# Sparse attention with routed experts: blocks of values on every fourth partition, exponentials written in the matching order, one GpSimd copy of values a tile

## The chip, the cores and the metric

One core of one Trainium2 chip. The metric is the device time of one execution in microseconds; the kernel before took 536.8 us (median of three runs, 534.89 to 540.84). A profiled execution gives the trace from which everything below is read.

## The reference, cut to what matters

Block-sparse attention over 4 batches of 8 heads, 768 positions and 64 channels, in blocks of 32 positions, and then a mixture of 8 experts in which each token goes to one expert:

```python
mask = np.abs(blk_i - blk_j) <= 1
mask = mask | (blk_i == 0) | (blk_j == 0) | (blk_i == n_blocks - 1) | (blk_j == n_blocks - 1)
for qb in range(n_blocks):
    for kb in sampled_blocks[qb]:
        mask[qb * 32:(qb + 1) * 32, kb * 32:(kb + 1) * 32] = True
scores = np.where(mask, scale * q @ k.T, -1e9)
attn = softmax(scores); out = attn @ v
...
e_idx = argmax(x @ w_gate + modality_bias[modality_id])
out[mask] = gate_w[mask, None] * (np.maximum(x[mask] @ w1[e], 0.0) @ w2[e])
```

So a middle block of queries sees eight blocks of keys and values: its own, its two neighbours, the first, the last, and three that are drawn (22 of the 24 blocks of queries are of this kind; the first and the last see everything).

## The kernel before, in words

**Halves and tiles.** The four batches are two halves of two. In each half the 22 middle blocks of queries are 11 tiles of two neighbouring blocks i and i+1 (i = 2m+1); tile g = 11 * half + m, so there are 22 sparse tiles. Blocks 0 and 23 of queries form the dense items. After the attention come groups of 256 tokens for the experts; that part starts at about 240 us and the change leaves it alone.

**Values of a tile.** `vbuf[g % 2]` holds 128 partitions by three columns of 1024 numbers (two batches, eight heads, 64 channels). A block of values is 32 rows of 4 KB and takes 32 partitions of one column. Column 1 is seen by both blocks of queries: i, 0, 23 and i+1. Column 0 belongs to the first block of queries: its three drawn blocks and i-1. Column 2 belongs to the second: i+2 and its three drawn blocks. Before, a block lay on 32 neighbouring partitions (0-31, 32-63, 64-95, 96-127).

**How they come there.** `fetch_v` (L484) issues, on SP's queue, the loads of i+2 (L495) and i+1 (L496), and for the first two tiles of a half the blocks 0 and 23 (L490); a half's first tile loads four more (L492, L493). `share_v` (L499) has GpSimd copy two blocks from the tile before: its i+1 becomes the new i-1, its i+2 the new i (two operations on 32 partitions by 1024 at L503). `fetch_own` (L515) loads the three drawn blocks of a block of queries, n = 0 into column 0 or n = 1 into column 2 (L520); the block numbers are registers read on SP (L512). Every load on SP waits for the one issued eight loads earlier, since eight counters are used in turn.

**Keys.** `share_k` (L461) has GpSimd copy the blocks of keys (L465, L469, and twelve copies at L481).

**One item.** An item is one block of queries (n) of one batch of one tile, four to a tile. Its steps: scores on TensorE (L532); mask and minimum on VectorE, which writes `y` (L540); two exponentials on ScalarE, which write `a` with the sum (L548, 256 numbers a partition each); four transposes on TensorE (L557); the copy to `at` on ScalarE (L562). After a tile's four items, TensorE multiplies with the values: `weigh_shared` (L574, matmuls at L579, column 1) and `weigh_own` (L582, L588, columns 0 and 2). A transposed row of `at` must lie on the same partition as its row of values. Then come division (L439 to L441), the transposes of the result (L595), its copy (L597) and the router (L605).

**What sets the order.** PE, DVE, ACT, POOL and SP run a hand-written order. A clock `t` counts items; `LAG` says how many places behind its item a step runs (`weigh_shared` 5 and `weigh_own` 7 behind the tile's last item), and within a place there are eight spots. `VL = (8, 1)`, `VS = (11, 7)` and `VG = ((9, 6), (10, 3))` (L69 to L71) place `fetch_v`, `share_v` and `fetch_own` n = 0 and n = 1: so many items behind the last item of tile g-2, and the spot. An engine's own instructions run in this order; where one waits, all behind it on that engine wait. The tile framework adds the waits that the buffers need.

Of the kernel before, what the change touches and what calls it, by code (L numbers as in the profile page):

```python
# [14 lines left out]
AF = mybir.ActivationFunctionType  # L15
ALU = mybir.AluOpType
# [4 lines left out]
P = 128  # L21
# [45 lines left out]
KL = (-2, 2)  # L67
QP = (-2, 2)
VL = (8, 1)  # L69
VS = (11, 7)  # L70
VG = ((9, 6), (10, 3))  # L71

DENSE_IN = ((19, 14, 30), (49, 38, 44))
Q_IN = 22
# [14 lines left out]
def attention_moe(ctx, tc, kD, qD, qH, v0, v1, blocks, modality, w_gate, bias, w1, w2, out):  # L89
    nc = tc.nc  # L90
# [28 lines left out]
    with ExitStack() as actx:  # L119
# [336 lines left out]
        def key_numbers(g):  # L456
            i = 2 * (g % NM) + 1
            picked[g] = nc.values_load_multi_w_load_instructions(
                rb_i[0:1, 3 * i:3 * i + 6], [ET.Pool], min_val=0, max_val=NB - 1, skip_runtime_bounds_check_because=NO_CHECK)[1]
# [24 lines left out]
        def fetch_v(m, half):  # L484
            i, g = 2 * m + 1, half * NM + m
            vg = vbuf[g % 2]
            vrow = vH[half].rearrange("(j s) b f -> s j (b f)", s=BLK)
            if m < 2:
                for n, j in ((0, 0), (1, NB - 1)):
                    nc.sync.dma_start(vg[32 + 32 * n:64 + 32 * n, 1, :], vrow[:, j, :])  # L490
            if m == 0:
                nc.sync.dma_start(vg[0:32, 1:3, :], vrow[:, i:i + 3:2, :])  # L492
                nc.sync.dma_start(vg[96:P, 0:2, :], vrow[:, i - 1:i + 2:2, :])  # L493
                return
            nc.sync.dma_start(vg[0:32, 2, :], vrow[:, i + 2, :])  # L495
            nc.sync.dma_start(vg[96:P, 1, :], vrow[:, i + 1, :])  # L496


        def share_v(m, half):  # L499
            g = half * NM + m  # L500
            new, old = vbuf[g % 2], vbuf[(g - 1) % 2]
            for r, c in ((slice(96, P), 0), (slice(0, 32), 1)):
                nc.gpsimd.tensor_scalar(new[r, c, :], old[r, c + 1, :], 1.0, 1.0, ALU.mult, ALU.mult)  # L503
            g = max(picked) + 1
            if g < 2 * NM:
                key_numbers(g)
# [8 lines left out]
        def fetch_own(m, half, n):  # L515
            i, g = 2 * m + 1, half * NM + m
            vg = vbuf[g % 2]
            vrow = vH[half].rearrange("(j s) b f -> s j (b f)", s=BLK)
            for k, reg in enumerate(own[g][3 * n:3 * n + 3]):
                nc.sync.dma_start(vg[32 * (k + n):32 * (k + n) + 32, 2 * n, :], vrow[:, bass.ds(reg, 1), :].rearrange("p j f -> p (j f)"))  # L520

# [21 lines left out]
        def exps(total, y, mn):  # L545
            a = work.tile([P, 768], F32, name="a", bufs=5)[:, 0:512].rearrange("p (u k) -> p u k", u=2)
            for u in range(2):
                nc.scalar.activation(a[:, u, :], y[:, u, :], AF.Exp, bias=mn[:, u:u + 1], scale=-1.0, accum_out=total[:, u:u + 1])  # L548
            return a


# [636 lines left out]
        for k, it in enumerate(sparse[0] + sparse[1]):  # L1188
            items.append(it)
            if k in DENSE_AFTER:  # L1190
                c = 2 * DENSE_AFTER.index(k)
# [5 lines left out]
        def side(t, f, place=7):  # L1197
            work_at.setdefault((t, place), []).append(f)
# [58 lines left out]
        for g in range(2 * NM):  # L1257
            half, m = divmod(g, NM)
            t = at["s", half, m, 0, 0]
            kl = lambda m=m, half=half: q_load(m, half)  # L1260
            qp = lambda m=m, half=half: share_k(m, half)
            vl = lambda m=m, half=half: fetch_v(m, half)
            vg = [lambda m=m, half=half, n=n: fetch_own(m, half, n) for n in range(2)]
            if g < 2:
                loads.update({f"kl{g}": kl, f"qp{g}": qp, f"vl{g}": vl, "vs1": lambda: share_v(1, 0), **{f"v{n}{g}": vg[n] for n in range(2)}})
                continue
            kt = last(g - 2) + KL[0]
            pt = max(kt, t + QP[0])
            vt = last(g - 2) + VL[0]
            side(kt, kl, KL[1])  # L1270
            side(pt, qp, QP[1])
            side(vt, vl, VL[1])
            if m:
                side(last(g - 2) + VS[0], lambda m=m, half=half: share_v(m, half), VS[1])
            for n in range(2):
                side(last(g - 2) + VG[n][0], vg[n], VG[n][1])

        st, done = {}, set()

        def do(op, it):  # L1280
# [29 lines left out]
            else:  # L1310
# [6 lines left out]
                elif op == "M":  # L1317
                    st[it] = masked(m, n, b, st[it])
                elif op == "X":
                    if (n, b) == (0, 0):  # L1320
                        sums[m, half] = small.tile([P, 4, 2], F32, name="sums", bufs=4)
                    st[it] = exps(sums[m, half][:, 2 * b + n, :], *st[it])
                elif op == "T":
                    st[it] = transposed(n, st[it])
                elif op == "A":
                    if n == 0:
                        ats[m, half, b] = work.tile([P, 16, 2, 32], F32, name="at", bufs=NAT)
                    copied(n, b, st.pop(it), ats[m, half, b])
                    if (n, b) == (1, HB - 1):
                        sums[m, half] = spread(sums[m, half])  # L1330
                elif (n, b) == (1, HB - 1):
                    if op == "W":
                        st[it] = bank()
                        weigh_shared(half * NM + m, st[it], [ats[m, half, b_] for b_ in range(HB)])
                    elif op == "V":
                        banks[m, half] = bank()
                        sum_rows(sums.pop((m, half)), banks[m, half])
                        weigh_own(half * NM + m, st[it], [ats[m, half, b_] for b_ in range(HB)])
                    elif op == "O":
                        new_tile(m, half)  # L1340
                        divide(st.pop(it), banks.pop((m, half))[:, 0:H], slice(0, P), H, xrs[m, half][:, 0:HD])
                    elif op == "Y":
                        turns[m, half] = turned(xrs[m, half])
                    elif op == "G":
                        end_tile(m, half)

        man = tc.manual_schedule(engines=MAN) if MAN else ExitStack()
        with man:
# [16 lines left out]
            while t < NI + LAG["s"]["G"] + 1 or fillers or slots_todo or choosers or early:  # L1365
                spot = 0
                for op in ORDER:
# [3 lines left out]
                    for kind in "ds":  # L1371
                        k = t - LAG[kind][op]
# [18 lines left out]
        total = nc.values_load(grp[0:1, 23:24], min_val=NG, max_val=NGMAX, skip_runtime_bounds_check_because=NO_CHECK)  # L1391
# [52 lines left out]
```

## Time and profile before

| what | value |
|---|---|
| median of three runs | 536.8 us (534.89 to 540.84) |
| the profiled execution's own time | 536.03 us |
| its span, first to last instruction | 534.3 us |
| granted TensorE clock, mean | 0.987 |
| busy over the span: PE, DVE, ACT, POOL | 514.9, 377.2, 335.2, 214.9 us |
| SP's transfers (queue q1) | 105.02 MB |
| drawn and shared blocks of values of 128 KB each | 180 transfers, 4.0 us from issue to landing (median) |

How to read it. PE is TensorE's matmuls and PEld its weight loads, which overlap; DVE is VectorE, ACT ScalarE, POOL GpSimd, SP the queue that issues the loads. Matmuls are pipelined and their ends are modelled, so a wait shows best as a gap between starts. "issue" as what ended a wait means that the profile shows nothing that the engine waited for. A window's row gives each engine's busy time and number of instructions in a stretch of the span, then the granted clock, the mean busy share of the sixteen DMA engines and what they moved.

### The profile page before, as it was taken

Reading aid. Unit: us, or ns where it says so; the run is one execution under the profiler, and the core shown is the slowest. Engines: PE = TensorE matmul, PEld = TensorE weight load, DVE = VectorE, ACT = ScalarE, POOL = GpSimd, SP = SyncE. Lnnn points to the kernel's source line nnn. Section 1 sums busy time; section 2 is a strip of 40 time slices with the busy share of each in tenths; the row PEclk is TensorE's granted clock in tenths of the full one; section 3 lists DMA queues with packets and bytes.
Section 4 is the critical chain, followed back from the end, with each engine's and each line's share of the span. In section 5 each row is a group of like instructions: output and inputs, shape, how many; then the busy total and the mean of one; then the engine's idle time right before and its main releaser. Section 6 shows DMA issues by size and latency. Waiting matters only on the chain.

```text
span 534.3 us, 19017 instructions
## 1 busy us (share of the span) xinstructions
PE 514.9 (96%) x7298; PEld 436.1 (82%) x7298; DVE 377.2 (71%) x1139; ACT 335.2 (63%) x765; POOL 214.9 (40%) x451
## 2 busy tenths in 40 slices
PE   7999999998999999899999999999999999999995
PEld 5667776766778777788989898998989899898984
DVE  7995698683788999867997656556565655656553
ACT  4689877884988878835456554546555454655552
POOL 3577685574468884323155022030302203030213
PEclk9999999997999999899999999999999999999998
DMA  7995887898846798965888686676758677675840
GB/s 278 339 234 153 238 244 224 243 229 223 232 126 194 198 231 252 274 193 200 238 288 303 227 261 200 237 252 202 244 177 261 203 227 242 213 246 180 257 155 23
DMA packets 49443, 119.44 MB, mean 224 GB/s; under 512 B 7744, under 2 KB 8128, under 8 KB 49344
## 3 DMA queue, kind: packets, MB, share of 16 engines
q1 hardware_dynamic: 45248, 105.02, 64.5%
q0 software_dynamic: 4096, 13.12, 7.3%
q8 instruction: 59, 0.97, 0.8%
q14 instruction: 40, 0.33, 0.2%
HBM read 105.52 MB, written 12.86 MB: 222 GB/s over the span
## 4 chain that ended last, share of the span: by engine, by line
issue 40%; PE 39%; DVE 7%; DMA 6%; POOL 6%; SPq 2%; ACT 1%; POOLq 0%; DVEq 0%; ACTq 0%
PE bank L557 7%; PE bank L532 6%; PE bank L579 4%; PE bank L588 4%; POOL slot L735 3%; DMA out<-slot,si 2%; DMA slot<-kD 2%; PE bank L605 2%; POOL out L789 2%; PE bank L595 2%; DVE y L540 2%; PE bank L753 1%; PE bank L769 1%; PE bank L770 1%; PE bank L768 1%
## 5 line engine op out<-in xcount | busy, mean ns | idle before, releaser
L724 DVE TENSOR_TENSOR slot<-slot 128x1024 fp32r<-128x1024 f32 x99 | 123.1, 1248 | 89.3 <-ACT slot L721 87.5
L721 ACT CAST slot<-slot 128x1024 fp32r<-128x1024 f32 x104 | 108.1, 1048 | 102.1 <-PE bank L754 52.1
L753 PE MATMUL bank<-slot 128*128 128x256 f32 x384 | 108.4, 282 | 0.0
L755 PE MATMUL bank<-slot 128*128 128x256 f32 x384 | 107.8, 281 | 0.0
L754 PE MATMUL bank<-slot 128*128 128x256 f32 x384 | 107.7, 280 | 0.0
L789 POOL DMA_INDIRECT out<-slot,si x20 | 25.4, 1270 | 178.6 <-ACT slot L785 175.6
L548 ACT ACTIVATE a<-y,mn 128x256 f32<-128x256 f32 x176 | 88.7, 511 | 7.7 <-DVE mn L540 7.6
L768 PE MATMUL bank<-slot 128*128 128x512 f32 x192 | 76.6, 399 | 0.0
L769 PE MATMUL bank<-slot 128*128 128x512 f32 x192 | 75.9, 395 | 0.0
L770 PE MATMUL bank<-slot 128*128 128x512 f32 x192 | 75.8, 395 | 0.0
L753 PEld LDWEIGHTS bank<-slot 128*128 128x128 f32 x384 | 72.3, 188 | 0.6
L754 PEld LDWEIGHTS bank<-slot 128*128 128x128 f32 x384 | 72.1, 188 | 0.4
L755 PEld LDWEIGHTS bank<-slot 128*128 128x128 f32 x384 | 72.2, 188 | 0.0
L540 DVE CUSTOM_DVE_ANT_1 y<-bank,smask 128x256 f32<-128x256 f32 x176 | 66.3, 416 | 0.6 <-PE bank L532 0.2
L481 POOL COPY slot<-slot 128x128 f32 x264 | 63.9, 294 | 0.0
L562 ACT COPY at<-bank 128x512 f32<-128x512 f32 x88 | 50.6, 576 | 12.8 <-PE bank L557 12.7
L557 PE MATMUL bank<-ident,a 128*128 128x128 f32 x352 | 52.8, 284 | 0.6 <-ACT a L400 0.5
L503 POOL TENSOR_SCALAR slot<-slot 32x1024 f32<-32x1024 f32 x40 | 41.9, 1048 | 28.0 <-PE bank L588 10.2
L532 PE MATMUL bank<-slot,q_raw 64*32 64x256 f32 x1408 | 48.8, 382 | 1.1 <-DMA q_raw<-qH 0.7
L770 PEld LDWEIGHTS bank<-slot 128*128 128x128 f32 x192 | 36.1, 188 | 8.4
L557 PEld LDWEIGHTS bank<-ident,a 128*128 128x128 f32 x352 | 38.9, 142 | 4.7 <-ACT a L548 0.8
L769 PEld LDWEIGHTS bank<-slot 128*128 128x128 f32 x192 | 36.1, 188 | 7.8 <-DVE slot L724 0.4
(302 smaller groups left out, 855.4 us busy)
## 6 DMA issues: line engine op xcount, KB each, us to landing
slot<-w SPq DMA_DIRECT2D x100, 512.0 KB, 4.0
slot<-v SPq DMA_DIRECT2D x180, 128.0 KB, 4.0
x_d<-xr SPq DMA_DIRECT2D x22, 256.5 KB, 5.3
q_raw<-qH SPq DMA_DIRECT2D x22, 256.0 KB, 4.8
slot<-v SPq DMA_DIRECT2D x16, 256.0 KB, 4.9
slot<-kD SPq DMA_DIRECT2D x13, 256.0 KB, 4.2
slot<-v SPq DMA_DIRECT2D x4, 768.0 KB, 11.9
slot<-w SPq DMA_DIRECT2D x10, 256.0 KB, 5.1
```

Source lines behind the costliest of these rows:

```text
L532: nc.tensor.matmul(sp[u][32 * pr:32 * pr + 32, b * 256:(b + 1) * 256], lhsT=q[r, b * NPAIR + pr, n, :], rhs=kv[r, s0:s0 + 8, b, pr, :], st ...
L540: nc.vector.tensor_tensor_reduce(y[:, u, :].rearrange("p (s f) -> p s f", s=8), sp[u][:, b * 256:(b + 1) * 256].rearrange("p (s f) -> p s ...
L548: nc.scalar.activation(a[:, u, :], y[:, u, :], AF.Exp, bias=mn[:, u:u + 1], scale=-1.0, accum_out=total[:, u:u + 1])
L557: nc.tensor.transpose(tp[:, k:k + P], a[:, u, c * P:(c + 1) * P], ident)
L721: nc.scalar.copy(h, s)
L724: (eng or (nc.gpsimd if n in POOL_SPLITS else nc.vector)).tensor_tensor(l, s, h.bitcast(F32), ALU.subtract)
L753: nc.tensor.matmul(o, lhsT=h[:, fs], rhs=xh[g % 2][:, c, :], start=c == 0 and f % 2 == 0, stop=False)
L754: nc.tensor.matmul(o, lhsT=h[:, fs], rhs=xl[g % 2][:, c, :], start=False, stop=False)
L755: nc.tensor.matmul(o, lhsT=l[:, fs], rhs=xh[g % 2][:, c, :], start=False, stop=c == 3 and f % 2 == 1)
L768: nc.tensor.matmul(o, lhsT=hh[0][:, f, ts_], rhs=h[:, fs], start=f == 0, stop=False)
L769: nc.tensor.matmul(o, lhsT=hh[0][:, f, ts_], rhs=l[:, fs], start=False, stop=False)
L770: nc.tensor.matmul(o, lhsT=hl[f // 4][:, f % 4, ts_], rhs=h[:, fs], start=False, stop=f == 7)
```

## The change

Three things, which belong together.

- **Place of a block.** A block of values takes partitions s, s+4, s+8, ... (s = 0 to 3) and not 32 neighbours. All value loads now write `vg[s:P:4, ...]`. Block i+1 lies on s = 3 of column 1, which is where i-1 of the next tile must lie in column 0.
- **Order of the exponentials.** For the transposed rows to meet these partitions, each exponential writes its 128-wide halves with the place within a block outside and the slot of the block inside: it reads `y` in order (slot, place) and writes element (slot, place) at 4 * place + slot. Consecutive elements of an instruction are so written 16 bytes apart, and the next slot fills the gaps.
- **Copy and loads.** `share_v` is one copy of all 128 partitions of column 1 of the tile before into column 0 of the new tile. Only the quarter s = 3 of it is used, the drawn blocks of n = 0 are loaded over the rest; so these loads must come behind the copy. Block i is no longer copied but loaded, in one transfer with i+2. `VS` moves to (9, 1), `VG` to (10, 5) for n = 0 and (9, 6) for n = 1.

Lines behind `fetch_v` have numbers lower by one or two in the changed kernel.

```diff
-VS = (11, 7)
-VG = ((9, 6), (10, 3))
+VS = (9, 1)
+VG = ((10, 5), (9, 6))
...
             if m < 2:
                 for n, j in ((0, 0), (1, NB - 1)):
-                    nc.sync.dma_start(vg[32 + 32 * n:64 + 32 * n, 1, :], vrow[:, j, :])
+                    nc.sync.dma_start(vg[1 + n:P:4, 1, :], vrow[:, j, :])
+            nc.sync.dma_start(vg[0:P:4, 1:3, :], vrow[:, i:i + 3:2, :])
             if m == 0:
-                nc.sync.dma_start(vg[0:32, 1:3, :], vrow[:, i:i + 3:2, :])
-                nc.sync.dma_start(vg[96:P, 0:2, :], vrow[:, i - 1:i + 2:2, :])
+                nc.sync.dma_start(vg[3:P:4, 0:2, :], vrow[:, i - 1:i + 2:2, :])
                 return
-            nc.sync.dma_start(vg[0:32, 2, :], vrow[:, i + 2, :])
-            nc.sync.dma_start(vg[96:P, 1, :], vrow[:, i + 1, :])
+            nc.sync.dma_start(vg[3:P:4, 1, :], vrow[:, i + 1, :])
...
             new, old = vbuf[g % 2], vbuf[(g - 1) % 2]
-            for r, c in ((slice(96, P), 0), (slice(0, 32), 1)):
-                nc.gpsimd.tensor_scalar(new[r, c, :], old[r, c + 1, :], 1.0, 1.0, ALU.mult, ALU.mult)
+            nc.gpsimd.tensor_scalar(new[:, 0, :], old[:, 1, :], 1.0, 1.0, ALU.mult, ALU.mult)
...
-                nc.sync.dma_start(vg[32 * (k + n):32 * (k + n) + 32, 2 * n, :], vrow[:, bass.ds(reg, 1), :].rearrange("p j f -> p (j f)"))
+                nc.sync.dma_start(vg[k + n:P:4, 2 * n, :], vrow[:, bass.ds(reg, 1), :].rearrange("p j f -> p (j f)"))
...
-                nc.scalar.activation(a[:, u, :], y[:, u, :], AF.Exp, bias=mn[:, u:u + 1], scale=-1.0, accum_out=total[:, u:u + 1])
+                nc.scalar.activation(a[:, u, :].rearrange("p (c f s) -> p c s f", c=2, s=4), y[:, u, :].rearrange("p (c s f) -> p c s f", c=2, s=4), AF.Exp, bias=mn[:, u:u + 1], scale=-1.0, accum_out=total[:, u:u + 1])
```

How the built program moves. GpSimd first, around the third tile (g = 2); `slot_100` and `slot_101` are the two buffers of values, `slot_98` and `slot_99` those of keys; a row of L465 opens the keys of a tile, L469 follows, and the twelve copies at L481 that close them are left out. Before:

```order
L465 TENSOR_SCALAR slot_99<-slot_98 128x512 [waits PE_49,Pool_49]
...
L465 TENSOR_SCALAR slot_98<-slot_99 128x512 [waits PE_49,Pool_49]
...
L469 TENSOR_SCALAR slot_98<-slot_109 128x2x2x64
...
L503 TENSOR_SCALAR slot_100<-slot_101 32x1024 [waits DMAHW2_49,PE_49,Pool_49]
L503 TENSOR_SCALAR slot_100<-slot_101 32x1024 [waits DMAHW1_49]
L458 TENSOR_LOAD rb_i_141
```

and with the change:

```order
L465 TENSOR_SCALAR slot_99<-slot_98 128x512 [waits PE_49,Pool_49]
...
L501 TENSOR_SCALAR slot_100<-slot_101 128x1024 [waits DMAHW3_49,DMAHW6_49,DMAHW2_49,DMAHW7_49,DMAHW0_49,PE_49]
L458 TENSOR_LOAD rb_i_141
L465 TENSOR_SCALAR slot_98<-slot_99 128x512 [waits Pool_49]
L469 TENSOR_SCALAR slot_98<-slot_109 128x2x2x64
```

One copy stands where two stood, and it stands ahead of the keys of tile 4, behind which the two stood.

SP's queue at the same tile, before (each L520 row is the first of three loads, the other two left out with the steps that set their registers):

```order
L495 DMA slot_100<-v0 32x1024 [waits DMAHW3_49,PE_49,Pool_49]
L496 DMA slot_100<-v0 32x1024 [waits DMAHW4_49]
L162 DMA slot_1163<-v1 128x512 [waits DMAHW5_49]
...
L520 DMA slot_100<-v0 32x1024 [waits DMAHW6_49]
...
L143 DMA q_raw_1231<-qH 128x512 [waits DMAHW1_49]
...
L520 DMA slot_100<-v0 32x1024 [waits DMAHW2_49]
```

and with the change:

```order
L491 DMA slot_100<-v0 32x2x1024 [waits DMAHW3_49,PE_49]
L495 DMA slot_100<-v0 32x1024 [waits DMAHW4_49]
L162 DMA slot_1162<-v1 128x512 [waits DMAHW5_49]
...
L518 DMA slot_100<-v0 32x1024 [waits DMAHW6_49]
...
L143 DMA q_raw_1244<-qH 128x512 [waits DMAHW1_49]
...
L518 DMA slot_100<-v0 32x1024 [waits DMAHW2_49,Pool_49]
```

As many loads as before, one of them of two blocks; the first of the second three (those of n = 0, which now come last) waits for GpSimd's copy, and the first of `fetch_v` no longer waits for GpSimd. TensorE's and VectorE's rows stand in the same order as before.

## The prediction

> **What bounds the kernel now.** I read the busy time by stage first (columns: the stretch, then PE, PEld, DVE, ACT and POOL busy with their counts, granted clock, DMA share, GB/s), then what PE waited for, then the groups.
>
> ```profile
> 28.00:60.00 32.00, 30.60 (x804) 23.21 (x796) 23.80 (x110) 28.00 (x94) 24.60 (x68) 1.00 0.74 204
> 60.00:90.00 30.00, 29.17 (x737) 21.77 (x718) 23.85 (x105) 23.64 (x77) 19.41 (x52) 1.00 0.79 230
> 90.00:120.00 30.00, 27.84 (x737) 21.60 (x733) 23.37 (x117) 25.90 (x84) 20.73 (x56) 1.00 0.91 238
> 120.00:150.00 30.00, 28.11 (x627) 21.53 (x630) 17.27 (x79) 20.93 (x67) 15.01 (x49) 0.89 0.74 205
> 150.00:180.00 30.00, 30.00 (x815) 23.41 (x805) 26.37 (x129) 26.10 (x86) 22.49 (x63) 1.00 0.65 186
> 180.00:210.00 30.00, 29.48 (x825) 23.21 (x826) 28.02 (x143) 25.89 (x83) 22.97 (x58) 1.00 0.83 226
> 210.00:228.00 18.00, 15.87 (x375) 13.38 (x361) 16.34 (x77) 14.41 (x40) 5.79 (x7) 0.91 1.01 270
> ```
>
> The change touches only these 200 us. PE is busy 191 of them, and all of 150 to 180: TensorE sets the pace. ACT is next, 52.0 of the 60 us from 150 to 210 (87%). POOL has slack everywhere.
>
> ```profile
> PE bank L579 <- issue: 3.2, 3, 2.7
> PE bank L588 <- issue: 2.2, 2, 1.8
> ...
> PE bank L579 <- POOL slot L503: 0.3, 1, 0.3
> ```
>
> In the whole stage PE waited 0.3 us, once, for `share_v`. Its longest waits, 2.7 and 1.8 us, are for nothing that the profile shows, in the middle of runs of equal matmuls. Here is the first of them, with the stretches at and behind both, and the instruction queue's row of 118 to 122 us:
>
> ```profile
> 121.60 0.69 PE L579 MATMUL bank<-slot,at 128*64 128x64 f32 x8 [2.65 <-issue]
> ```
>
> ```profile
> 119.00:122.00 3.00, 0.40 (x8) 0.40 (x10) 2.28 (x13) 1.20 (x5) 2.83 (x7) 0.82 0.97 264
> 122.00:129.00 7.00, 7.00 (x107) 4.95 (x107) 0.37 (x2) 3.62 (x11) 2.66 (x12) 0.59 0.99 256
> ...
> 217.00:220.00 3.00, 1.93 (x42) 1.66 (x41) 2.84 (x13) 2.73 (x7) 2.82 (x3) 0.99 1.03 261
> 220.00:224.00 4.00, 4.00 (x49) 3.88 (x48) 2.96 (x9) 2.14 (x7) 1.49 (x2) 0.58 1.04 288
> ```
>
> ```profile
> q8 instruction: 1, 0.02, 2.0%
> ```
>
> The DMA engines are full there (share 0.97 to 1.04) and a packet of code is under way, so I read them as late code; this is argued, not shown. Behind each the granted clock is 0.59 and 0.58, which costs 7 x 0.41 + 4 x 0.42 = 4.6 us more. The two places cost 2.7 + 1.8 + 4.6 = 9.1 us together.
>
> **GpSimd's part.** The rows of the groups between 28 and 240 us:
>
> ```profile
> L548 ACT ACTIVATE a<-y,mn 128x256 f32<-128x256 f32 x176 | 88.7, 511 | 7.7 <-DVE mn L540 7.6
> L562 ACT COPY at<-bank 128x512 f32<-128x512 f32 x88 | 50.6, 576 | 12.8 <-PE bank L557 12.7
> L503 POOL TENSOR_SCALAR slot<-slot 32x1024 f32<-32x1024 f32 x40 | 41.9, 1048 | 28.0 <-PE bank L588 10.2 <-DMA slot<-x_d,gi_e 5.5 <-issue 5.2
> L597 ACT COPY xT<-bank 128x512 f32<-128x512 f32 x24 | 14.2, 592 | 7.9 <-PE bank L595 7.9
> L465 POOL TENSOR_SCALAR slot<-slot 128x512 f32<-128x512 f32 x19 | 11.8, 621 | 22.0 <-PE bank L532 10.8 <-PE bank L430 5.8 <-PE bank L572 4.4
> ```
>
> Forty copies of 1048 ns become twenty. A copy of 128 partitions by 512 takes 621 ns, so one of 128 by 1024 lies between 1048 (as on 32 partitions) and 2 x 621 = 1242 ns. I take 1.05 us: 42 us of POOL become 21. On the path this is the 0.3 us that PE waited. Its cover is POOL's slack (7 us of 30 at the fullest); without it all 21 us would show.
>
> **VectorE's part.** A copy on GpSimd holds up small operations of VectorE. Two rows of the timeline, and the same operation elsewhere:
>
> ```profile
> 173.32 2.17 POOL L503 TENSOR_SCALAR slot<-slot 32x1024 f32<-32x1024 f32 x2
> ```
>
> ```profile
> 174.50 1.02 DVE L355 TENSOR_SCALAR r<-r 128x2 int32<-128x2 int32 x1
> ```
>
> ```profile
> 206.20 0.16 DVE L355 TENSOR_SCALAR r<-r 128x2 int32<-128x2 int32 x1
> ```
>
> That is 0.86 us lost to one copy. At up to one such loss a copy, twenty fewer copies return 0 to 17 us to VectorE, over 200 us. It is not the bound (28.02 of 30 us at most) and PE never waits long for it, so I take 0.5 us off the time, of bounds 0 and 2.
>
> **SP's queue and the added wait.** As many transfers, twenty of them 256 instead of 128 KB: 2.6 MB more on 200 us, at 186 to 270 GB/s some 10 to 14 us of the DMA engines' time spread over the stage. The share is 0.65 to 0.91 before 210 us, so it is hidden but where the engines are full already (near 120 and 210 to 228 us, with one to three tiles' loads): 0 to 2 us, taken as 0.5. The new wait is that of the n = 0 loads for the copy. Queued behind it on SP are two more drawn blocks, the result's store and the next `fetch_v`; `weigh_own` waits for the first. The rows of one tile on POOL:
>
> ```profile
> 180.91 2.18 POOL L503 TENSOR_SCALAR slot<-slot 32x1024 f32<-32x1024 f32 x2
> 183.77 0.62 POOL L465 TENSOR_SCALAR slot<-slot 128x512 f32<-128x512 f32 x1 [0.68 <-PE bank L572]
> ...
> 185.19 2.88 POOL L481 COPY slot<-slot 128x128 f32 x12
> 188.16 2.17 POOL L503 TENSOR_SCALAR slot<-slot 32x1024 f32<-32x1024 f32 x2
> ```
>
> A tile takes 7.25 us, an item 1.8. The keys end at 188.07 and the copy starts at once; with the change it stands ahead of the next keys, and it needs the same `weigh_own` of tile g-2 as `fetch_v` does. SP has six transfers to issue between, so the copy of 1.05 us is done first. Were it a whole set of keys late (183.77 to 188.07, 4.3 us), the loads would still have their 4.0 us to land: they stand 5 items, 9 us, ahead of `weigh_own`. Cost 0, bound 1.
>
> **ScalarE's part, the large unknown.** 176 exponentials write their numbers 16 bytes apart. No row shows this on ACT. From below: the copy at L562 writes runs of 32 numbers with gaps and takes 576 ns, the contiguous one at L597 592, so jumps as such are free, and nothing makes an exponential faster than 511 ns. From above, every number taking the time of two:
>
> ```profile
> L400 ACT ACTIVATE a<-bank,nb__301 128x512 f32<-128x512 f32 x1 | 0.7, 687 | 0.0
> ...
> L401 ACT ACTIVATE a<-bank,nb__301 128x256 f32<-128x256 f32 x1 | 0.5, 467 | 0.0
> ```
>
> 256 more numbers cost 220 ns, so at most +0.22 us each, +39 us in all. The nearest rows that step over numbers are small ones of VectorE, from single lines of the source: a write of 8 numbers 36 bytes apart (L1090) and its contiguous neighbour; and 24 numbers 12 bytes apart, read twice and written (L264), with contiguous ones of 8 and 64.
>
> ```profile
> L1089 DVE TENSOR_SCALAR narrow<-taken x1: 171/171/171, 235.1 to 235.1; 128x8 f32<-128x8 f32 x1
> ```
>
> ```profile
> L1090 DVE TENSOR_SCALAR start<-taken x1: 168/168/168, 235.1 to 235.1; 128x8 f32<-128x8 f32 x1
> ```
>
> ```profile
> L264 DVE TENSOR_TENSOR t<-t x3: 193/194/195, 6.5 to 15.0; 128x24 f32<-128x24 f32 x3
> ```
>
> ```profile
> L1087 DVE TENSOR_TENSOR taken<-ce,ce x1: 154/154/154, 234.9 to 234.9; 128x8 f32<-128x8 f32 x1
> ```
>
> ```profile
> L1114 DVE TENSOR_TENSOR start<-before_e,gnum x1: 224/224/224, 255.6 to 255.6; 128x64 f32<-128x64 f32 x1
> ```
>
> The write alone is free (168 against 171). The other took 194 where the line from 154 to 224 gives 174: 20 ns over 24 numbers, but with two inputs that step too. The exponential reads contiguously and only its writes step, so it is nearest to L1090: I take +0, and keep +0.22 for the range. The Trainium skill speaks against this change here: "SBUF — State Buffer", Specifications, says that a line is 16 bytes and that accesses keep full bandwidth only with two or more hits to a line. Here every write would be the first to a new line; L264 fits that rule and L1090 does not, and by it the result is the first rival below.
>
> **Sum.** Own time of the profiled execution 536.0 - 0.3 (PE's wait) - 0.5 (VectorE) + 0.5 (loads) + 0 (exponentials, added wait) = 535.7. It lay 0.8 below the median, so against medians **536 us**, with 533 to 539 as its own range.
>
> **Rival 1, slower: the spaced writes cost.** Each exponential +0.22 us. From 150 to 210 us, 60 / 7.25 = 8.3 tiles hold 66 exponentials: ACT 52.0 + 14.5 = 66.5 in 60 us, so ACT sets the pace and the stretch grows by 6.5 us if ACT never idles, by 10.7 if it is busy 94%. The other 110 add 24 us to 112.9 of 140 us: with the uneven windows 0 to 9 us. So 7 to 20, taken as 15: **551 us**. The mechanism decides from about +0.1 us each: then ACT has 52.0 + 6.6 = 58.6 of 60, and at 94% the loss is 2 to 5 us (540). For it: L264. Against: L1090.
>
> **Rival 2, faster: loads over all partitions end sooner and code is no longer late.** In the full stretches above a share of one moves 256 to 288 GB/s. The experts' stage, whose loads cover 128 partitions, gives more:
>
> ```profile
> 283.00:534.00 251.00, 245.33 (x1594) 221.87 (x1592) 148.48 (x159) 128.75 (x160) 54.83 (x46) 0.99 0.66 217
> ```
>
> 217 / 0.66 = 329. If blocks spread over all partitions ran at that rate, the values' bytes (9/8) would take 9/8 x 272 / 329 = 0.93 of their time, and the fetches at 119 and 216 us could be in time: -9.1 at best, taken as -7: **529 us**. Against it: a few per cent of load need not free a fetch, and a place of full load can move as well as vanish. The Trainium skill ("SBUF — State Buffer", Door 1: The DMA port swizzle) has 32 neighbouring partitions reach 8 of 16 ports; every fourth one would reach all by its formula, which agrees with 329 against 272.
>
> **How the numbers follow.** Forecast (no change, 533 to 539) 0.42. Rival 1 in full 0.30 and in part, or with loads that cost more than taken, 0.10. Rival 2 0.18. One per cent, about what a measurement of this kernel can tell from no change, is 5.4 us: faster 0.17, same 0.43 (with the mildest of each rival), slower 0.40. The range must take in most of rival 1 and the nearer half of rival 2: 529 to 554.
>
> **What would show it.** Right: the exponentials' mean stays within 500 to 530 ns; twenty copies of 128x1024 near 1.05 us; PE's row full from 150 to 210 us; SP's wait for GpSimd under 1 us in all. Wrong: a mean above 600 ns, PE waiting for ScalarE's exponentials and a tile's period over 8 us (rival 1); no wait named "issue" above 1 us and a clock of 1.00 in every stretch (rival 2); `weigh_own` waiting for loads (the added wait).

## The result, and the profile after

The changed kernel takes **583.1 us** (median of six runs, 579.56 to 584.58); the kernel before took 537.05 beside it. The ratio is 1.088 (95% interval 1.084 to 1.092): 46 us slower, far outside the forecast's range. In one run below (`e18_slab_copy_pool`) two of four executions were disturbed, so it has no interval and its other two are named.

One row for the whole stage from 28 to 240 us (columns as in the prediction: PE, PEld, DVE, ACT, POOL busy, granted clock, DMA share, GB/s), of the kernel before

```profile
28.00:240.00 212.00, 202.67 (x5061) 159.07 (x5045) 166.46 (x788) 169.13 (x533) 133.57 (x350) 0.98 0.79 218
```

and of the changed one, with the two of its stretches that were fullest before:

```profile
28.00:240.00 212.00, 178.34 (x4269) 135.71 (x4268) 125.18 (x634) 159.91 (x461) 97.60 (x298) 0.90 0.61 183
```

```profile
150.00:180.00 30.00, 25.53 (x546) 18.86 (x542) 16.43 (x74) 22.35 (x66) 11.29 (x34) 0.97 0.71 209
180.00:210.00 30.00, 27.79 (x728) 22.19 (x731) 22.48 (x121) 24.64 (x71) 15.69 (x48) 0.97 0.51 159
```

In the same 212 us TensorE gets through 4269 matmuls where it did 5061, stands still for 34 us, and is granted 0.90 of its clock and not 0.98. No engine is full, the DMA engines less so than before (0.61 against 0.79). So this is a stage of waits. What PE waited for, then POOL, then SP (total, times, longest):

```profile
PE bank L530 <- POOL slot L481: 38.1, 12, 6.5
...
PE bank L586 <- DMA slot<-v: 2.0, 2, 1.1
```

```profile
POOL slot L501 <- DMA slot<-v: 65.8, 9, 12.7
```

```profile
SPq L518 <- POOL slot L501: 9.2, 7, 2.4
```

Scores (L530) wait 38.1 us for the twelve copies of keys (L481). Before, all that waited for L481 on TensorE was 0.3 us of its weight loads. With PE's longer busy time at the lower clock (528.6 against 514.9 us, 13.7 more) and the 3.2 + 2.2 = 5.4 us of unexplained stops that are gone, it makes 38.1 + 13.7 - 5.4 = 46.4 of the span's 581.8 - 534.3 = 47.5 us. One tile shows the chain; SP's queue, POOL and PE:

```profile
182.13 0.65 SPq L491 DMA_DIRECT2D slot<-v  x1
```

```profile
185.38 1.04 POOL L501 TENSOR_SCALAR slot<-slot 128x1024 f32<-128x1024 f32 x1 [6.34 <-PE bank L530]
186.89 0.62 POOL L465 TENSOR_SCALAR slot<-slot 128x512 f32<-128x512 f32 x1 [0.46 <-POOL slot L501]
187.47 0.91 POOL L469 TENSOR_SCALAR slot<-slot 128x256 f32<-128x256 f32 x2
188.33 2.88 POOL L481 COPY slot<-slot 128x128 f32 x12
```

```profile
187.03 0.60 PE L555 MATMUL bank<-ident,a 128*128 128x128 f32 x4
189.84 0.45 PE L530 MATMUL bank<-slot,q_raw 64*32 64x256 f32 x8 [2.21 <-POOL slot L481]
```

POOL is idle for 6.34 us before the copy. The releaser named there, a matmul at L530, cannot be it: the copy reads nothing from there. The copy starts 3.25 us after SP issued L491, the load of blocks i and i+2 into the *same* buffer, and this load takes 3.2 to 4.6 us to land (median 3.6). In the built program the copy does wait for the counter of that load, and all twenty copies start 3.2 to 6.3 us after the issue of their own tile's L491, none ahead of it. It writes column 0 and the load columns 1 and 2, but the load's access, every fourth partition by two columns, counts as overlapping. So the copy stands behind a load that SP issues only after `weigh_own` of tile g-2, and the keys stand behind the copy.

The groups of the two operations that the change makes anew:

```profile
L546 ACT ACTIVATE a<-y,mn 128x256 f32<-128x256 f32 x176 | 121.9, 780 | 2.7 <-DVE mn L538 2.4
L501 POOL TENSOR_SCALAR slot<-slot 128x1024 f32<-128x1024 f32 x20 | 21.3, 1063 | 126.4 <-DMA slot<-v 65.8 <-PE bank L603 11.7 <-DMA q_raw<-qH 10.4
```

An exponential went from 511 to 780 ns, more than the upper bound of +0.22 us. The copy costs what was taken (1.06 us).

### The profile page after: what moved, and what is told of

Its sections match the earlier page's. It is cut to its first block, busy times and chain, and to the rows that moved or that the text cites. A ratio compares the mean times of both kernels' runs of the same rounds, so it can differ in the third digit from the quotient of the medians.

```text
span 581.8 us, 19033 instructions
## 1 busy us (share of the span) xinstructions
PE 528.6 (91%) x7298; PEld 445.0 (76%) x7298; DVE 367.1 (63%) x1139; ACT 355.9 (61%) x765; POOL 194.0 (33%) x431
## 4 chain that ended last, share of the span: by engine, by line
issue 41%; PE 28%; DMA 11%; POOL 8%; SPq 5%; POOLq 3%; DVE 2%; ACT 0%; ACTq 0%; DVEq 0%
DMA slot<-v 6%; PE bank L530 5%; PE bank L555 4%; PE bank L577 3%; DMA out<-slot,si 3%; PE bank L586 2%; POOL slot L733 2%; POOLq L458 2%; POOL slot L481 2%; SPq L518 2%; PE bank L603 2%; POOL out L787 2%; PE bank L751 1%; PE bank L767 1%; PE bank L768 1%
## 5 line engine op out<-in xcount | busy, mean ns | idle before, releaser
L546 ACT ACTIVATE a<-y,mn 128x256 f32<-128x256 f32 x176 | 121.9, 780 | 2.7 <-DVE mn L538 2.4
L530 PE MATMUL bank<-slot,q_raw 64*32 64x256 f32 x1408 | 54.3, 418 | 38.6 <-POOL slot L481 38.1
L751 PEld LDWEIGHTS bank<-slot 128*128 128x128 f32 x384 | 72.2, 188 | 0.6
L752 PEld LDWEIGHTS bank<-slot 128*128 128x128 f32 x384 | 72.1, 188 | 0.4
L753 PEld LDWEIGHTS bank<-slot 128*128 128x128 f32 x384 | 72.2, 188 | 0.0
L560 ACT COPY at<-bank 128x512 f32<-128x512 f32 x88 | 52.0, 592 | 30.9 <-PE bank L555 30.9
L530 PEld LDWEIGHTS bank<-slot,q_raw 64*32 64x32 f32 x1408 | 23.4, 113 | 54.0 <-POOL slot L481 41.6
L481 POOL COPY slot<-slot 128x128 f32 x264 | 63.6, 293 | 0.0
L501 POOL TENSOR_SCALAR slot<-slot 128x1024 f32<-128x1024 f32 x20 | 21.3, 1063 | 126.4 <-DMA slot<-v 65.8
L555 PE MATMUL bank<-ident,a 128*128 128x128 f32 x352 | 55.0, 292 | 0.3 <-ACT a L400 0.3
L555 PEld LDWEIGHTS bank<-ident,a 128*128 128x128 f32 x352 | 40.6, 147 | 4.4 <-ACT a L546 0.8
L768 PEld LDWEIGHTS bank<-slot 128*128 128x128 f32 x192 | 36.1, 188 | 8.4
```

What stands on the lines that cost most here:

```text
L481: nc.gpsimd.tensor_copy(kg[:, k + k // 3 * 6, b * P:(b + 1) * P].rearrange("p (c f) -> p c f", c=2), kd[half * HB + b][:, :, bass.ds(reg, ...
L530: nc.tensor.matmul(sp[u][32 * pr:32 * pr + 32, b * 256:(b + 1) * 256], lhsT=q[r, b * NPAIR + pr, n, :], rhs=kv[r, s0:s0 + 8, b, pr, :], st ...
L546: nc.scalar.activation(a[:, u, :].rearrange("p (c f s) -> p c s f", c=2, s=4), y[:, u, :].rearrange("p (c s f) -> p c s f", c=2, s=4), AF. ...
L555: nc.tensor.transpose(tp[:, k:k + P], a[:, u, c * P:(c + 1) * P], ident)
L751: nc.tensor.matmul(o, lhsT=h[:, fs], rhs=xh[g % 2][:, c, :], start=c == 0 and f % 2 == 0, stop=False)
L752: nc.tensor.matmul(o, lhsT=h[:, fs], rhs=xl[g % 2][:, c, :], start=False, stop=False)
```

## The experiments

**First round: the copy's wait against the exponentials.** Theory A: two costs, the copy's wait and the exponentials. Theory B: the exponentials alone. The edits, together or apart:

```diff
-            nc.sync.dma_start(vg[0:P:4, 1:3, :], vrow[:, i:i + 3:2, :])
+            for c in (1, 2):
+                nc.sync.dma_start(vg[0:P:4, c, :], vrow[:, i + 2 * c - 2, :])
...
-                nc.scalar.activation(a[:, u, :].rearrange("p (c f s) -> p c s f", c=2, s=4), y[:, u, :].rearrange("p (c s f) -> p c s f", c=2, s=4), AF.Exp, bias=mn[:, u:u + 1], scale=-1.0, accum_out=total[:, u:u + 1])
+                nc.scalar.activation(a[:, u, :], y[:, u, :], AF.Exp, bias=mn[:, u:u + 1], scale=-1.0, accum_out=total[:, u:u + 1])
```

> The changed kernel with its load of two columns (slots 1 and 2, blocks i and i+2) written as two loads of one column each. GpSimd's copy of column 0 then waits only for the old tile's values and no longer for the new tile's load; the spaced exponentials stay. Theory A (two costs: the copy waits for the new tile's own load, with the keys of a later tile queued behind it on GpSimd, and the exponentials take 0.27 us more each): TensorE's waits for the keys (38 us after the change) go to under 8 us, GpSimd's wait of the copy for a load (65.8 us) to under 20, and the time to about 553 us (545 to 562): what is left over is the exponentials. Theory B (the exponentials alone set the pace, and every wait of GpSimd and TensorE follows from that lateness): the time stays at 575 us or more.

Measured: 560.1 us, ratio 1.044 (1.038 to 1.050).

> The changed kernel with the exponentials written in place order as before the change, so that the rows of weights meet values of other keys: the output is not the reference's; the number and shape of all other instructions are the same. Theory A: the exponentials go back to some 510 ns, the copy's wait and TensorE's waits for the keys stay at 25 us or more, and the time is about 567 us (560 to 578). Theory B: the waits for the keys go with the exponentials, and the time is 534 to 542 us.

Measured: 582.3 us, 1.081 (1.075 to 1.088), as the change itself.

> Both edits: the two-column load written as two loads, and the exponentials written in place order (the output is not the reference's, since rows of weights meet values of other keys). Theory A and theory B both have it near the kernel before: 533 to 540 us. Anything above 545 us means that a third cost of the change is still there, in the loads onto every fourth partition or in the order of GpSimd's work; under 531 us that the freed GpSimd time or the loads are worth something.

Measured: 559.7 us, 1.042 (1.036 to 1.048), as with the first edit alone.

> The kernel before with the one line of the exponentials as the change has it, and all else left (the output is not the reference's, since rows of weights meet values of other keys). Each exponential should take some 780 ns in place of 511. Theory A: about 551 us (545 to 558), with no wait of TensorE for keys. Theory B: 575 us or more, with TensorE's waits for keys as after the change.

Measured: 536.9 us, 0.997 (0.993 to 1.001).

Theory B falls, and so does half of A: the exponentials cost nothing, three times over. Why 0.27 us more on each of 176 is free shows in the distance of starts. Before, two of one item and what follows:

```profile
151.95 0.51 ACT L548 ACTIVATE a<-y,mn 128x256 f32<-128x256 f32 x1 [0.37 <-DVE mn L540]
...
152.46 0.49 ACT L548 ACTIVATE a<-y,mn 128x256 f32<-128x256 f32 x1
...
152.95 0.56 ACT L562 COPY at<-bank 128x512 f32<-128x512 f32 x1
```

and in `e4_exp_only`:

```profile
153.00 0.79 ACT L548 ACTIVATE a<-y,mn 128x256 f32<-128x256 f32 x1 [0.89 <-DVE mn L540]
...
153.62 0.78 ACT L548 ACTIVATE a<-y,mn 128x256 f32<-128x256 f32 x1
...
154.22 0.61 ACT L562 COPY at<-bank 128x512 f32<-128x512 f32 x1
154.71 0.60 ACT L597 COPY xT<-bank 128x512 f32<-128x512 f32 x1
```

The rows overlap. From start to start an exponential takes 0.61 us where it took 0.50: +0.11, not +0.27. An item's two and its copy need 0.62 + 0.60 + 0.49 = 1.71 us of ScalarE, and TensorE's item takes 1.8, so it just fits.

The split load took away what it should. In `e1` every one of the twenty copies starts 1.9 to 8.4 us *ahead* of its own tile's loads. Here is one, with the first two of these loads:

```profile
187.61 1.10 POOL L502 TENSOR_SCALAR slot<-slot 128x1024 f32<-128x1024 f32 x1 [3.79 <-DMA slot<-v]
```

```profile
191.95 1.15 SPq L492 DMA_DIRECT2D slot<-v  x2
```

The waits for keys are 4.1 us after 38.1, and 23 us are left that the change's other parts must explain:

```profile
PE bank L587 <- DMA slot<-v: 12.2, 8, 2.7
PE bank L531 <- POOL slot L481: 4.1, 3, 2.0
```

TensorE now waits for values in the multiplication with the drawn blocks. (Lines behind `fetch_v` stand one or two apart from kernel to kernel.)

**Second round: the copy's place against the stepped loads.** Theory C puts the rest on the chain through the copy; D on SP, which takes longer to issue a load to stepped partitions (every fourth one). The four edits: no copy but a tenth block loaded (`e5`); neighbouring partitions (`e6`); and the places alone, in the kernel before (`e7`, `e8`).

```diff
-            nc.sync.dma_start(vg[3:P:4, 1, :], vrow[:, i + 1, :])
+            for c in (0, 1):
+                nc.sync.dma_start(vg[3:P:4, c, :], vrow[:, i + 2 * c - 1, :])
...
-            nc.gpsimd.tensor_scalar(new[:, 0, :], old[:, 1, :], 1.0, 1.0, ALU.mult, ALU.mult)
```

> The kernel of the first run (the load of two columns split) with GpSimd's copy taken out and the block that it carried, i-1, loaded as a tenth block; exponentials and places stay as in the change. That run is still 23 us above the kernel before, and TensorE waits 12 us there for values in the multiplication with the drawn blocks. Theory C (the copy of the whole column is a link in a chain: the multiplication of tile g-2, then the copy, then on the one side GpSimd's next keys, on the other the drawn loads of n = 0, which must come behind it): with the link gone, the waits for keys are under 1 us, those for values under 4, and the time is 534 to 542 us. Theory D (the loads onto every fourth partition take SP 478 instead of 316 ns to issue, and so the drawn blocks are late): one more load makes it no better than the first run, 557 us or more.

Measured: 572.9 us, 1.071 (1.065 to 1.078). Worse than `e1` by 13 us for twenty more loads; TensorE's waits for values are 15.1 us.

```diff
-                nc.sync.dma_start(vg[k + n:P:4, 2 * n, :], ...)
+                nc.sync.dma_start(vg[32 * (k + n):32 * (k + n) + 32, 2 * n, :], ...)
```

(and so for the other loads).

> The run with both edits (load split, exponentials in place order), with all loads of blocks put back onto 32 neighbouring partitions; the copy of the whole column and the order stay (the output is not the reference's: one of the blocks that the multiplication meets is another's). Theory C: 553 to 562 us, as with stepped loads. Theory D: SP issues a load in some 320 ns again, and the time is 534 to 542 us.

Measured: 541.4 us, 1.010 (1.002 to 1.018). The expectation's remark on the output was mistaken: neighbouring partitions and place order belong together, so this run computes the same as the kernel before.

```diff
-VS = (11, 7)
+VS = (9, 1)
```

> The kernel before with its two copies of 32 partitions at the change's place (nine items behind, ahead of the next keys, not eleven items behind them); nothing else. Loads of the drawn blocks need not come behind these copies. It prices GpSimd's side of the chain alone: the keys of the next tile behind a copy that waits for the multiplication of tile g-2. Theory C: TensorE's waits for keys of 3 to 8 us and a time of 540 to 550 us. Theory D: 534 to 540 us.

Measured: 534.5 us, 0.998 (0.994 to 1.002).

```diff
-VG = ((9, 6), (10, 3))
+VG = ((10, 5), (9, 6))
```

> The kernel before with all three places as in the change: the copies nine items behind, and the drawn loads of n = 0 behind those of n = 1. Against the run with the copies alone moved it prices the order of the loads: under both theories no more than 3 us beyond that run, since these copies and loads do not touch the same rows and no load waits for GpSimd.

Measured: 535.7 us, 1.001 (0.998 to 1.005).

C falls. The change's order costs nothing (`e7`, `e8`), and the whole-column copy with its place in the chain little (`e6`, 1.010). What makes 18 us is the step over partitions (559.7 against 541.4). SP's issues in `e1_two_loads` (shortest/median/longest ns):

```profile
L519 SPq DMA_DIRECT2D slot<-v x132: 472/478/1860, 25.9 to 248.2; - x132
...
L496 SPq DMA_DIRECT2D slot<-v x20: 584/586/1230, 35.4 to 242.9; - x20
...
L143 SPq DMA_DIRECT2D q_raw<-qH x22: 328/574/1402, 16.6 to 216.7; - x22
```

and in `e6_slabs`:

```profile
L519 SPq DMA_DIRECT2D slot<-v x132: 315/316/2358, 25.2 to 229.3; - x132
...
L496 SPq DMA_DIRECT2D slot<-v x20: 311/413/1768, 32.6 to 223.7; - x20
...
L143 SPq DMA_DIRECT2D q_raw<-qH x22: 328/422/1012, 17.1 to 198.0; - x22
```

A stepped load holds SP 160 ns longer, and the load of queries right behind one, itself unchanged, goes from 422 to 574 ns. The Trainium skill, "Perfetto Trace Analysis", DMA Instruction — HWDGE (DVE, Sync), says that an issue's row holds the wait for the descriptor generator and its work, not the data; these rows agree as far as the data go (478 ns, where the same loads land after 3.0 us). Per tile SP issues six drawn loads, three others, a load of queries and a store of results: 5.6 us by the medians in `e1`, 3.9 in `e6`. The gaps between its rows add about 2.8 in both: 1.57 while block numbers are read into registers, 0.18 ahead of each further drawn load, some 0.1 elsewhere. That is an estimate of 8.4 us against 6.7, and TensorE's tile takes 7.25. SP's loads of values are made to wait for others only some 12 us in all of `e1`, about 0.5 us a tile: SP itself is what is late.

**Third round: SP relieved.** The three loads of `fetch_v` on another queue, or the queries' loads and the results' stores:

```diff
-                nc.sync.dma_start(vg[0:P:4, c, :], vrow[:, i + 2 * c - 2, :])
+                nc.scalar.dma_start(vg[0:P:4, c, :], vrow[:, i + 2 * c - 2, :])
```

(`nc.gpsimd` in `e11`; in `e12` the same on the queries' load and the results' store, in `e15` those on `nc.gpsimd`). `e9` is the changed kernel with neighbouring partitions and place order, the edits shown above.

> The changed kernel with blocks back on 32 neighbouring partitions and exponentials in place order (the two belong together, so the output stays the reference's), and with the load of two columns kept as one transfer. With the runs so far it fills the square of loads (one of two columns, or two of one) by place (every fourth partition, or neighbours). Theory D, now with two terms (the copy's wait for its own tile's load, and SP's longer issue of stepped loads): the copy's wait costs by itself what it cost on stepped partitions, so 541 + 23 = 564 us (555 to 570), with TensorE's waits for keys of 25 us or more. Rival (the wait bites only because SP is already late): 541 to 548 us and waits for keys under 10 us.

Measured: 540.4 us, 1.016 (1.007 to 1.025). It does not test what it was meant to. On neighbouring partitions the framework sees that columns 0 and 1 to 2 are apart: the copy waits there for L491 of the *old* tile, not of its own. Its copies start up to 3.5 us ahead of the issue of their own L491 and never more than 0.02 us behind it, so the wait is not in this kernel.

> The kernel of the first run (stepped loads, the load of two columns split) with the three loads of blocks that are not drawn issued by ScalarE and not by SP. Theory D as a matter of SP's own queue (nine loads a tile, each of 0.6 us, in one line with registers and waits): with three of them elsewhere the drawn loads come some 1.8 us a tile earlier, TensorE's 12 us of waits for values go to under 4, and the time falls from 560 to 538 to 550 us, less what ScalarE loses by standing still. Rival (what makes the descriptors is shared by both queues, or the loss is not SP's): 555 us or more.

Measured: 567.7 us, 1.056 (1.044 to 1.069).

> The same three loads issued by GpSimd, whose descriptors are made by software. Theory D as SP's queue: SP is relieved as in the run on ScalarE's queue, 538 to 550 us if GpSimd's queue has room, and more if the loads hold up the keys behind them. Rival (not SP's queue): 555 us or more, with SP's issue of the drawn loads still at 478 ns and as close together as before.

Measured: 538.7 us, 1.012 (1.003 to 1.021).

> The kernel of the first run with the loads of the queries and the stores of the results (two transfers a tile, on all partitions, 0.4 to 0.6 us of SP each) issued by ScalarE; all loads of values stay on SP. Theory D as SP's queue: about 1 us a tile freed of some 10, so 547 to 555 us. Rival (shared by both queues, or not SP's): 557 us or more.

Measured: 582.8 us, 1.094 (1.080 to 1.108).

GpSimd's queue takes the loss away. ScalarE's does not (`e10`, whose interval meets that of `e1`), or adds to it (`e12`). In `e10` the wait has moved:

```profile
PE bank L578 <- ACT at L561: 13.3, 13, 2.9
```

ScalarE's copies come late. The three issues take it 2 x 0.48 (L492) and 0.70 us (L496) a tile, 1.65 together; with four items of 1.71 that is an estimate of 8.5 us against the tile's 7.25. ScalarE also has to stand still where such a load waits for `weigh_own`; no run separates the two. In `e12` ScalarE's issues are short (340 ns for the queries, 332 for the results), but SP's loads of values now wait for the landing of ScalarE's transfers:

```profile
SPq L519 <- DMA x_d<-xr: 16.6, 4, 5.4
...
SPq L496 <- DMA x_d<-xr: 8.3, 2, 4.2
...
SPq L492 <- DMA x_d<-xr: 5.1, 1, 5.1
```

These are 30.0 us for the stores of results alone. In `e1` there is no such entry. TensorE's waits for values in `weigh_own` rise from 12.2 us there to 23.0. The eight counters are used in turn by both queues, and a load waits for the transfer that last took its counter, on whichever queue that stands. The Trainium skill, "Perfetto Trace Analysis", DMA Optimizations, says that balancing DMAs over sync, scalar and GpSimd may help where descriptor generation is the limit; here it held for GpSimd and not for ScalarE.

**Fourth round: is the copy's wait a cost of its own?** `fetch_v` is given to GpSimd in the changed kernel (`e13`), in `e5` (`e14`) and in the kernel before without its copies (`e16`):

```diff
-            nc.sync.dma_start(vg[0:P:4, 1:3, :], vrow[:, i:i + 3:2, :])
+            nc.gpsimd.dma_start(vg[0:P:4, 1:3, :], vrow[:, i:i + 3:2, :])
...
-            for r, c in ((slice(96, P), 0), (slice(0, 32), 1)):
-                nc.gpsimd.tensor_scalar(new[r, c, :], old[r, c + 1, :], 1.0, 1.0, ALU.mult, ALU.mult)
```

> The changed kernel with the loads of the blocks that are not drawn issued by GpSimd; the load of two columns stays one transfer, and the copy still waits for it. Theory D (SP's queue is full, and everything else follows from its lateness): 536 to 545 us, TensorE's waits for keys under 8 us. Rival (two causes: the copy that waits for its own tile's load costs by itself, even when SP is in time): 548 to 562 us, with 15 us or more of TensorE's waits for keys.

Measured: 583.3 us, 1.089 (1.083 to 1.095), the change's own time, with SP relieved.

> The run without a copy (ten blocks loaded, on every fourth partition), with the four loads that are not of drawn blocks issued by GpSimd. On SP that run took 572.9 us. Theory D: with SP back at six loads of values a tile, 533 to 539 us. Rival (it is the number of stepped loads, wherever they are issued): 560 us or more.

Measured: 539.2 us, 1.003 (1.000 to 1.007).

> The first run (560.1 us) with the loads of the queries and the stores of the results issued by GpSimd. From ScalarE's queue the same two cost 23 us more, where a load of values on SP could come to wait for a store that stood in ScalarE's queue, as the eight counters are shared by both. Theory D (a dose of some 1 us of SP's time a tile, between nothing and the 1.8 us of the three loads that brought 538.7 us): 543 to 554 us. Rival (relief of SP does nothing unless it is the loads of values): 557 us or more.

Measured: 542.2 us, 1.010 (1.006 to 1.013).

> The kernel before (neighbouring partitions, exponentials in place order) without its copies: ten blocks loaded, the four that are not drawn by GpSimd's queue, the six drawn by SP. It keeps what the change was to bring to GpSimd and leaves out what it cost on SP. Theory D: no loss, 531 to 538 us, with SP less busy than before; a gain of over 1% (under 530 us) would mean that copies or SP's queue had cost something before, which the profile of before does not show.

Measured: 556.3 us, 1.036 (1.031 to 1.040).

`e13` differs from `e11` only in the one load of two columns, and takes 44.5 us more by the medians (41 by the ratios, since the two ran on different chips). Its waits, PE's and SP's:

```profile
PE bank L530 <- POOL slot L481: 29.3, 14, 5.1
```

```profile
SPq L518 <- POOL slot L501: 45.8, 17, 6.5
```

The rival named in its expectation holds in kind, though its 548 to 562 us did not: there are two causes, each enough by itself. All four on every fourth partition, in us with the ratio to the kernel before:

| | SP issues nine loads a tile | six, the others by GpSimd |
|---|---|---|
| copy waits for its own tile's load | 583.1 (1.088) | 583.3 (1.089) |
| it does not | 560.1 (1.044) | 538.7 (1.012) |

The wait alone makes 44.5 us, SP's queue alone 21.4 (41 and 17 by the ratios), and both together not the sum but the wait's own 45. That the stalls of the wait leave SP time to catch up is how I read it; no run shows it by itself.

SP's relief does work in doses. By the estimate above (6.7 us a tile in `e6`, `e11` and `e14`; 7.4 in `e15`; 8.4 in `e1`; 9.0 in `e5`) the ratios are 1.010, 1.012 and 1.003; 1.010; 1.044; 1.071. As near as this estimate tells, the loss sets in a little behind the tile's 7.25 us.

**Last round: `e16`, 18 us above what was expected.** Ten blocks, four by GpSimd: 539.2 us on every fourth partition, 556.3 on neighbours. The stage's row of `e14`, and of `e16`:

```profile
28.00:240.00 212.00, 199.33 (x5042) 155.15 (x5024) 154.80 (x788) 188.61 (x533) 139.40 (x402) 0.98 0.78 239
```

```profile
28.00:240.00 212.00, 191.79 (x4752) 147.44 (x4731) 149.84 (x733) 162.27 (x519) 134.01 (x399) 0.95 0.89 224
```

More bytes in less share of the DMA engines: 239 / 0.78 = 306 GB/s at a full share against 224 / 0.89 = 252. In `e17` all ten blocks are SP's; `e18` is `e6` with `fetch_v` on GpSimd's queue.

```diff
-                nc.gpsimd.dma_start(vg[0:32, c, :], vrow[:, i + 2 * c - 2, :])
+                nc.sync.dma_start(vg[0:32, c, :], vrow[:, i + 2 * c - 2, :])
```

> The kernel before without copies and with ten blocks loaded, all ten by SP; blocks on neighbouring partitions. With four of the ten on GpSimd's queue it took 556.3 us, and TensorE stood still nine times for 1.3 to 3.0 us in the middle of runs of equal matmuls, for nothing that the profile shows, with the DMA engines' share near one. Theory F (ten blocks on neighbouring partitions fill the DMA engines, and code comes late): 548 to 560 us, with 10 us or more of such waits. Rival G (loads to neighbouring partitions from GpSimd's queue are what hurts): 537 to 545 us and such waits under 6 us.

Measured: 551.6 us, 1.024 (1.017 to 1.032), but only 4 us of unexplained stops.

> Blocks on neighbouring partitions, one copy of the whole column, the change's order and nine blocks, three of them loaded by GpSimd (from SP all nine took 541.4 us). Theory F: 538 to 546 us, as nine blocks fill the DMA engines no more than from SP. Rival G: 550 us or more.

Measured: 542.4 and 548.1 us, beside 538.7 for the kernel before.

The times speak for F, the fill of the DMA engines, in `e17`: ten blocks cost on either queue. They do not clear the queue: `e18` lies at F's upper end or above it, and with nine blocks its share of the DMA engines is 0.88, where `e6` has 0.83. F's second number fails too. The unexplained stops are 20.4 of TensorE's 23.7 us of waits in `e16`, and 4.0 of 19.9 in `e17`, where waits for values are 5.3. That the stops are late code is not shown, and the cause of the 18 us of `e16` stays open. No version is measurably faster than the kernel before.

## Why the prediction was wrong

**The step that failed: "Cost 0, bound 1" for the added wait.** It reasoned that the copy "needs the same `weigh_own` of tile g-2 as `fetch_v` does" and is done while SP issues. That is not all it needs. It also waits for `fetch_v`'s own load to land, 3.25 us after its issue at 182.13. The rows of GpSimd's order in the section on the change name five DMA counters ahead of the copy; I did not ask which loads they stood for. And I priced the wait only for what is behind it on SP. "With the change it stands ahead of the next keys" was in the text, yet the keys behind it got no price. Measured alone: 41 to 45 us.

**The second failed step: "+0.5 (loads)", bounds 0 to 2.** It counted the bytes on the DMA engines and took a load's issue as unchanged. SP's issue went from 316 to 478 ns, and by the estimate above SP's time a tile from under the tile's 7.25 us to over it. Measured alone: 17 to 21 us, hidden in the result behind the first.

**Rival 1 named the right number for the wrong row.** The bound of +0.22 us was passed (+0.27) and the sign "a mean above 600 ns" came, and it cost nothing: the duration of a row is not the distance to the next. The taken 0 was right for the time, not for the reason given, and so it was luck. L1090 was no guide, since 16-byte steps on ScalarE do cost +0.11 us from start to start. This lies at the rival's own threshold of "about +0.1 us each", so it stayed just free. The 16-byte line of the Trainium skill ("SBUF — State Buffer", Specifications) agrees with the longer rows (780 against 511 ns).

**Rival 2 was right on the transfers and wrong on the time.** The drawn blocks landed in 2.9 us on every fourth partition instead of 3.9 (medians). The stops named "issue" are gone from the changed kernel, but there the DMA engines are less full anyway. In `e14`, where their share is 0.78 (0.79 before), the stops are there again (8.6 us, 5.6 before), so spreading the blocks does not remove them. With both costs removed (`e14`, 1.003) nothing is gained: TensorE is the bound, busy 199 of the stage's 212 us.

**The small terms.** The copy's 1.05 us was right (1.06), and taking 21 us off GpSimd brought nothing, as said. The 0.3 us of PE's wait went and 38.1 came. VectorE's 0.5 us is below what any run here can tell.

**The signs.** PE's row of 150 to 180 us fell from 30.00 to 25.53, SP's wait for GpSimd reached 9.2 us, and `weigh_own` waited for loads, 2.0 us in the changed kernel and 12.2 once the first cost was out of the way.

## What to carry to other kernels

When an instruction moves up an in-order queue, list every semaphore in front of it, ask which transfer each stands for, and price what is queued behind it on its own engine, not only on the one that waits for it. A queue that issues transfers has a time per tile of its own: add up its issues and register reads and set the sum against the tile, above all when an access pattern changes. Test two suspected costs in a square; in sequence, one can hide the other.

## What the runs showed of the hardware

- A load of 32 partitions by 4 KB holds SP 316 ns to neighbouring partitions and 478 to every fourth; right behind other loads (L496) 413 and 586. GpSimd's queue took about 0.5 us for either (medians of 489 to 505 ns and 526 to 542).
- With stepped loads the stage moved more at an equal share of the DMA engines: 297 to 315 GB/s at a full share (the changed kernel, `e1`, `e11`, `e14`), against 252 to 276 on neighbouring partitions (the kernel before, `e6`, `e16` to `e18`).
- An exponential of 256 numbers written 16 bytes apart shows 780 ns against 511, but 0.61 us against 0.50 from start to start.
- A load that SP issues can wait for a store that ScalarE issued, since both take their turns on the same eight counters (30.0 us in `e12`).
- One access of two columns on stepped partitions ties in a third column that it does not touch (the copies of the changed kernel start 3.2 us or more behind it); two accesses of one column each do not (`e1`), nor does one of two columns on neighbouring partitions (`e9`). This is the framework's doing, not the chip's.
